# A linear-attention and SwiGLU kernel whose whole instruction order is made by the builder's detailed timeline simulation

## The chip, the cores and the metric

The kernel runs on one core of a Trainium2 chip. The metric is device time in microseconds of one execution. TensorE (PE; its weight loads are PEld), VectorE (DVE), ScalarE (ACT) and GpSimd (POOL) each work through their own instructions in the order in which the builder has put them; SyncE (SP) issues most of the DMA transfers, also in order. An instruction that waits holds up everything behind it on its engine.

## The reference, cut to what matters

The input x has 2048 rows of 576. It is normalised by row, and two branches of it are multiplied.

```python
xn = _layernorm(x)
# A: linear attention, 32 heads of 18
q, k, v = split(xn @ wqkv)
phi = lambda t: concat(softmax(t @ w_phi), softmax(-(t @ w_phi)))
o = (phi(q) @ (phi(k).T @ v)) / (phi(q) @ phi(k).sum() + 1e-6)
s = o @ wo
# B: SwiGLU with 4608 hidden columns
g = silu((silu(xn @ w_gate) * (xn @ w_up)) @ w_down)
return x + s * g
```

All of it is in float32. Times below are microseconds from the start of the span of the profiled execution.

## The kernel before, in words

Every float32 operand is split into a rounded high part (ScalarE, L60) and the rest (VectorE, L61), and a product is three matmuls, high by high, high by low and low by high, in the fp32r type. The gate and up products and the down products are made by Strassen's scheme with seven products of half-size blocks.

The kernel has these stages.

- The head (0 to about 66). Sixteen tiles of x (`xn`) are loaded by SyncE (L177), normalised (statistics L186, scaling L201 on ScalarE and L204 on VectorE), transposed on TensorE (`tp`, L216) and copied out of PSUM on ScalarE and VectorE (`X`, L218 to L224; the last copy, L224, is `xr`). The feature weights are folded (`tp`, L249). SyncE also stores sums of X to DRAM for later (`a_dram`, L337).
- The key stage (about 66 to 230): the projections of keys (`p2`) and values (`vx`, `vy`, `vw`, copied out in L429), the softmax parts (L313 to L321) and the state `kvp`.
- The query stage (about 240 to 490): sixteen query tiles (`p2`, written by `q_tile`), each with its softmax parts and denominators on VectorE (L604 to L614). For each pair of tiles `numer` works through five groups of heads: transposes into `pt` (L625), their split into `ph` and `pl`, the product with the state into `po` (L631), and its split into `oh` and `ol`; `project` multiplies these with wo into `p` (L651).
- The two main passes over the hidden columns (about 490 to 1010 and 1010 to 1580), one for each half of the rows. A unit is 128 hidden columns: seven products of seven matmuls of 512 columns each into `px`, `py` and `pw` (L758). Two snapshots of px are taken by ScalarE (`s`, L787) and added to pw by VectorE (L792) before the next product may write into the same bank. Between the products the down products (`pd`, L875, 288 columns) of earlier units are put in by calls of `fill`. Unit weights are split on the chip in pass 0 and stored to `w_dram` (L736), and read back from there in pass 1 (L732); the tail rows of the weights come from `t_dram` into two tiles in turn, `wt0` and `wt1` (L741).

Some hidden columns are treated early, by `early_tile` (`pe`, L94), as work for TensorE beside the head, the key stage and the query stage; their results (`h_dram`) are loaded again in the main passes.

What sets the order: the program text gives instructions in one order, and the builder of the tile context then lays out all engines' instructions by simulating the program with a cost for each, its dependences and priorities (`tc.high_priority`) and with the constraints of `tc.issue_after`. In the kernel before, that simulation uses a short estimate of each instruction. The ring of hand-offs in the query stage reads:

```python
for s in range(2):
    for j, e in enumerate(es):
        nc.tensor.transpose(pt[0:w, s, j * P:(j + 1) * P], e[:, s * D + o:s * D + o + w], ident)
split(ph[0:w], pl[0:w], pt[0:w])
for k, (a, p) in enumerate(((KVH, ph), (KVL, ph), (KVH, pl))):
    for s in range(2):
        nc.tensor.matmul(po[0:w], a[0:w, 2 * g + s, 0:w], p[0:w, s], start=k + s == 0, stop=k + s == 3)
split(oh[0:w, g], ol[0:w, g], po[0:w])
```

and the part of a unit with snapshots:

```python
product(xp, w, 5, S2, False, False)
s2 = snap(xp)
fill()
product(xp, w, 2, S3, False, False)
s3 = snap(xp)
add(wp, s3)
fill()
```

## Time and profile before

| what | us |
|---|---|
| median of three runs | 1603.73 |
| the runs | 1602.67 to 1605.22 |
| profiled execution | 1603.6 |
| its span, first to last instruction | 1601.7 |
| TensorE busy in the span | 1590.1 |
| VectorE busy | 1176.5 |
| ScalarE busy | 724.9 |
| GpSimd busy | 663.7 |

How to read the rows: a row of the timeline has start, length, engine, line, operation, output and inputs with sizes, the count of instructions that were merged into it, and in brackets how long the engine sat idle before it and what released it. A row of a group has its count, then busy time and the mean length of one in ns, then idle time before it with what ended it. A row of windows has the stretch, its length, then busy time (and count) of PE, PEld, DVE, ACT and POOL, the granted clock, the share of the DMA engines and GB/s. Matmuls overlap, so the time that one takes of the queue is the distance between two starts, not the length of a row.

### The profile page before, as it was taken

What the parts mean: (1) busy time and instruction counts of PE and PEld (TensorE: products, weight loads), DVE (VectorE), ACT (ScalarE), POOL (GpSimd) and SP (SyncE); (2) the same over time, 40 slices, a digit from 0 to 9 for tenths busy, and PEclk for the clock granted to TensorE, in tenths of its full rate; (3) what the DMA queues carried; (4) which work ended last, traced back from release to release, by engine and by line L of the source; (5) the groups of instructions that cost most, each with busy time, mean ns of one, the idle gap of its engine ahead of it and who ended that gap; (6) DMA issues with size and microseconds to landing.
All of it is one profiled execution on the core that took longest, in us unless ns stands there. A gap on an engine that the chain in (4) does not pass through costs nothing.

```text
span 1601.7 us, 25319 instructions
## 1 busy us (share of the span) xinstructions
PE 1590.1 (99%) x9415; PEld 1420.7 (89%) x9415; DVE 1176.5 (73%) x1729; ACT 724.9 (45%) x1404; POOL 663.7 (41%) x714
## 2 busy tenths in 40 slices
PE   9999999999999999999999999999999999999998
PEld 6899998999988888888888888888888888888887
DVE  7777769889866778987777778635667656666577
ACT  5633345444435654544444444455343333333334
POOL 3676662434115535544535445223324324133133
PEclk9999999999999999999999999999999999999999
DMA  9522243436438454455545453874545565556435
GB/s 313 189 81 80 91 145 115 126 108 189 127 132 280 164 192 165 164 180 189 179 163 201 171 180 124 325 229 139 163 138 146 183 193 158 171 181 187 143 117 178
DMA packets 123181, 268.29 MB, mean 168 GB/s; under 512 B 12978, under 2 KB 54066, under 8 KB 121778
## 3 DMA queue, kind: packets, MB, share of 16 engines
q1 hardware_dynamic: 107612, 244.73, 46.5%
q0 software_dynamic: 3552, 12.59, 2.7%
q10 hardware_dynamic: 11894, 9.35, 1.8%
q8 instruction: 74, 1.21, 0.3%
q14 instruction: 49, 0.40, 0.1%
HBM read 167.53 MB, written 99.09 MB: 166 GB/s over the span
## 4 chain that ended last, share of the span: by engine, by line
PE 92%; DVE 3%; POOL 2%; DMA 2%; ACT 1%; issue 1%; SPq 0%; ACTq 0%; DVEq 0%; POOLq 0%
PE pd L875 25%; PE px L758 24%; PE pw L758 12%; PE py L758 6%; PE p L94 6%; PE pe L94 5%; PE p L651 4%; PE kvp L330 2%; PE po L631 2%; PE vx L418 1%; PE pt L625 1%; POOL slo L363 1%; PE vy L94 1%; PE vx L94 1%; DMA wst<-in_A_w_qk 0%
## 5 line engine op out<-in xcount | busy, mean ns | idle before, releaser
L875 PEld LDWEIGHTS pd<-dw,hh 128*128 128x128 f32 x3012 | 424.0, 188 | 22.2 <-ACT pd L922 1.5
L875 PE MATMUL pd<-dw,hh 128*128 128x288 f32 x3012 | 438.5, 295 | 1.4 <-ACT pd L922 0.7
L758 PE MATMUL px<-X,w 128*128 128x512 f32 x1512 | 386.5, 390 | 0.0
L758 PEld LDWEIGHTS px<-X,w 128*128 128x128 f32 x1512 | 274.6, 188 | 49.1 <-ACT s L787 2.3
L758 PE MATMUL pw<-X,w 128*128 128x512 f32 x744 | 190.7, 392 | 0.0
L758 PEld LDWEIGHTS pw<-X,w 128*128 128x128 f32 x744 | 138.6, 188 | 29.4
L792 DVE TENSOR_TENSOR s<-pw,s 128x512 f32<-128x512 f32 x126 | 86.4, 687 | 97.7 <-ACT s L787 86.4
L1029 DVE TENSOR_TENSOR acc<-pd,acc 128x576 f32<-128x576 f32 x128 | 96.2, 753 | 76.9 <-PE pd L875 76.4
L787 ACT COPY s<-px 128x512 f32<-128x512 f32 x126 | 73.6, 584 | 156.7 <-PE px L758 156.7
L61 DVE TENSOR_TENSOR hh<-ha,hh 128x512 fp32r<-128x512 f32 x140 | 111.3, 821 | 21.8 <-ACT hh L60 21.4
L60 ACT CAST hh<-ha 128x512 fp32r<-128x512 f32 x140 | 82.7, 619 | 87.6 <-PE pd L875 74.3
L1001 POOL TENSOR_TENSOR hb<-hb 128x512 f32<-128x512 f32 x34 | 46.5, 1367 | 160.6 <-DVE hb L804 159.6
L94 PE MATMUL pe<-X,wh 128*128 128x512 f32 x340 | 107.0, 395 | 0.3 <-ACT wh L64 0.3
L61 DVE TENSOR_TENSOR w<-ld,w 128x512 fp32r<-128x512 f32 (+1 forms) x96 | 80.5, 839 | 34.2 <-ACT w L60 32.9
L758 PE MATMUL px<-X,wt 128*128 128x512 f32 x252 | 98.1, 389 | 0.0
L758 PE MATMUL py<-X,w 128*128 128x512 f32 x378 | 97.0, 391 | 0.0
L988 POOL TENSOR_TENSOR h<-ha,hb 128x512 f32<-128x512 f32 x34 | 44.6, 1313 | 124.2 <-DVE ha L808 94.1
L1014 POOL TENSOR_TENSOR ha<-ha 128x512 f32<-128x512 f32 x34 | 52.6, 1563 | 97.2 <-DVE hh L61 97.2
L60 ACT CAST w<-ld 128x512 fp32r<-128x512 f32 (+1 forms) x96 | 52.8, 550 | 87.3 <-POOL ld L746 57.2
L812 ACT COPY py<-px 128x512 f32<-128x512 f32 x63 | 36.0, 572 | 103.8 <-PE px L758 74.9
L743 POOL TENSOR_TENSOR ts<-ld 128x256 f32<-128x256 f32 x32 | 27.6, 864 | 127.0 <-issue 71.4
L758 PEld LDWEIGHTS py<-X,w 128*128 128x128 f32 x378 | 67.8, 188 | 10.7
(286 smaller groups left out, 3256.1 us busy)
## 6 DMA issues: line engine op xcount, KB each, us to landing
w_dram<-w SPq DMA_DIRECT2D x90, 512.0 KB
w<-w_dram SPq DMA_DIRECT2D x90, 512.0 KB
wt<-t_dram SPq DMA_DIRECT2D x62, 336.0 KB
ld<-in_B_w_gu SPq DMA_DIRECT2D x32, 512.0 KB
rt<-in_B_w_down SPq DMA_DIRECT2D x33, 288.0 KB
rb<-in_B_w_down SPq DMA_DIRECT2D x33, 288.0 KB
w_dram<-w SPq DMA_DIRECT2D x30, 256.0 KB
w<-w_dram SPq DMA_DIRECT2D x30, 256.0 KB
```

What stands on the lines that cost most here:

```text
L60: nc.scalar.copy(hi, src)
L61: nc.vector.tensor_sub(lo, src, hi)
L94: last = nc.tensor.matmul(ps, l, r, start=n == 0, stop=n == len(pairs) - 1)
L651: nc.tensor.matmul(ps[:, 0:HALF], a[0:w, g, jc], bw[0:w, g, n], start=k == 0, stop=k == 3 * NG - 1)
L758: nc.tensor.matmul(ps, l, r, start=first and n == 0, stop=last and n == len(mm) - 1, skip_group_check=True)
L787: snaps.append(nc.scalar.copy(t, ps))
L792: nc.vector.tensor_add(t, ps, t)
L875: nc.tensor.matmul(ps, l, r, start=first and n == 0 and m == 0, stop=n == len(hs) - 1 and m == 2, skip_group_check=True)
L988: sub(s, g["h"][0][0], g["h"][0][1])
L1001: nc.gpsimd.tensor_add(a21, a21, g["h"][1][1])
L1014: sub(a12, a12, g["h"][0][0])
L1029: nc.vector.tensor_add(a2, pd[:, :, 0:HALF], a2)
```

## The change

One argument is given to the tile context:

```diff
-    with tile.TileContext(nc) as tc:
+    with tile.TileContext(nc, schedule_with_timeline_sim=True) as tc:
```

With it the builder makes the order of every engine with its detailed timeline simulation in place of its short estimate of each instruction. What is computed, the instructions' kinds and sizes, the tiles and their buffers stay.

First place: TensorE at the end of the head. `tp_620` is the last transposed piece of x, `p2_795` the first key projection, `pe_740` an early tile. Before:

```order
L216 MATMUL tp_620<-ident_89,xn_427 128x128
L216 MATMUL tp_620<-ident_89,xn_429 128x128
L94 MATMUL pe_740<-X13_67,wh_397 128x512
L94 MATMUL pe_740<-X13_67,wl_398 128x512
L94 MATMUL pe_740<-X13_67,wh_397 128x512 x2
L94 MATMUL pe_740<-X13_67,wl_398 128x512
L94 MATMUL pe_740<-X13_67,wh_397 128x512 x2
L94 MATMUL p2_795<-KVWH_101,X10_64 128x288
```

And TensorE there now:

```order
L94 MATMUL pe_740<-X13_67,wl_398 128x512
L94 MATMUL pe_740<-X13_67,wh_397 128x512 x2
L216 MATMUL tp_609<-ident_89,xn_423 128x128
...
L216 MATMUL tp_620<-ident_89,xn_423 128x128
L216 MATMUL tp_620<-ident_89,xn_425 128x128
L216 MATMUL tp_620<-ident_89,xn_427 128x128
L216 MATMUL tp_620<-ident_89,xn_429 128x128
L94 MATMUL p2_795<-KVWH_101,X10_64 128x288
```

The early matmuls stood between the last transposes and the first key projection; now they stand ahead of the transposes. On SyncE the store of X11 to `a_dram` now stands ahead of the loads of xn_423, xn_425, xn_427 and xn_429, and was behind them; on ScalarE casts into `KVWH` (from tp_288) and `wh_275` now stand between the L218 and the L224 copies of the first block, and were behind them.

Second place: TensorE in the query stage, at the projection `p_4383` (`oh_4191` and `ol_4192` are its inputs, `po_4211` and on the products of the groups with the state). Before:

```order
L651 MATMUL p_4383<-WOH_2467,oh_4191 128x288
L651 MATMUL p_4383<-WOL_2468,oh_4191 128x288
L94 MATMUL pe_5146<-X00_60,wh_5071 128x512
L94 MATMUL pe_5146<-X01_61,wh_5071 128x512
L94 MATMUL pe_5146<-X01_61,wl_5072 128x512
L631 MATMUL po_4211<-ph_4217,KVH_2399 126x256 x2
L631 MATMUL po_4211<-ph_4217,KVL_2400 126x256 x2
L631 MATMUL po_4211<-pl_4218,KVH_2399 126x256 x2
```

And now:

```order
L651 MATMUL p_4383<-WOH_2467,oh_4191 128x288
L651 MATMUL p_4383<-WOL_2468,oh_4191 128x288
L631 MATMUL po_4211<-ph_4217,KVH_2399 126x256 x2
L631 MATMUL po_4211<-ph_4217,KVL_2400 126x256 x2
L631 MATMUL po_4211<-pl_4218,KVH_2399 126x256 x2
L651 MATMUL p_4383<-WOH_2467,ol_4192 128x288
L651 MATMUL p_4383<-WOH_2467,oh_4191 128x288
L651 MATMUL p_4383<-WOL_2468,oh_4191 128x288
L625 MATMUL pt_4462<-ident_89,e_4312 126x128
```

The early matmuls have gone from between the steps of the ring. Over the whole stage: before, early matmuls stand between the query tiles throughout, and 96 of them behind the last one (`p2_4333`); now the last of them stands ahead of the tenth tile, `p2_3529`, and the six tiles behind that one (`p2_3747`, `p2_3797`, `p2_4015`, `p2_4065`, `p2_4283`, `p2_4333`) and all groups behind them have none.

Third place: TensorE in pass 0, around the unit whose bank is `px_8386` (`px_8513` is the next unit's, `pd_8437` a down product). Before:

```order
L758 MATMUL px_8386<-X10_5247,w2_8205 128x512 x6
L758 MATMUL px_8386<-X10_5247,wt1_5223 128x512
L875 MATMUL pd_8437<-dw_8335,hh_8337 128x288 x3
L875 MATMUL pd_8437<-dw_8335,hh_8343 128x288 x3
L875 MATMUL pd_8437<-dw_8335,hh_8337 128x288 x3
L875 MATMUL pd_8437<-dw_8335,hh_8343 128x288 x3
L758 MATMUL px_8386<-X12_5252,w2_8209 128x512 x6
L758 MATMUL px_8386<-X12_5252,wt1_5223 128x512
L758 MATMUL px_8513<-X00_60,w2_8365 128x512 x4
L758 MATMUL px_8386<-X03_63,w1_8213 128x512 x6
```

And now:

```order
L758 MATMUL px_8513<-X00_60,wt0_5222 128x512
L758 MATMUL py_8387<-X01_61,w2_8196 128x512 x6
L758 MATMUL py_8387<-X01_61,wt1_5223 128x512
L758 MATMUL px_8386<-X10_5247,w2_8205 128x512 x6
L758 MATMUL px_8386<-X10_5247,wt1_5223 128x512
L758 MATMUL px_8386<-X12_5252,w2_8209 128x512 x6
L758 MATMUL px_8386<-X12_5252,wt1_5223 128x512
L758 MATMUL px_8386<-X03_63,w1_8213 128x512 x6
L758 MATMUL px_8386<-X03_63,wt1_5223 128x512
L758 MATMUL pw_8388<-X11_5257,w2_8209 128x512 x6
```

The down product and the next unit's first product no longer stand between the three px products; that first product is now done ahead of them, and down products come earlier in the pass.

## The prediction

> **What bounds the kernel now.** I read the page first, then busy time by windows, then TensorE's waits.
>
> ```profile
> span 1601.7 us, 25319 instructions
> PE 1590.1 (99%) x9415; PEld 1420.7 (89%) x9415; DVE 1176.5 (73%) x1729; ACT 724.9 (45%) x1404; POOL 663.7 (41%) x714
> PEclk9999999999999999999999999999999999999999
> PE 92%; DVE 3%; POOL 2%; DMA 2%; ACT 1%; issue 1%; SPq 0%; ACTq 0%; DVEq 0%; POOLq 0%
> ...
> 250.00:460.00 210.00, 209.96 (x1410) 191.84 (x1409) 186.57 (x293) 96.10 (x167) 58.48 (x120) 1.00 0.41 124
> 500.00:1010.00 510.00, 509.27 (x2824) 451.28 (x2823) 405.45 (x576) 255.41 (x508) 256.99 (x246) 1.00 0.51 175
> 1010.00:1580.00 570.00, 570.00 (x3140) 503.52 (x3139) 363.68 (x518) 228.01 (x444) 169.73 (x138) 1.00 0.57 177
> ...
> PE tp L216 <- DVE xn L204: 1.2, 2, 0.7
> PE p L94 <- ACT xr L224: 0.6, 1, 0.6
> ```
>
> TensorE (first figure after each window's length) is busy 1590.1 of 1601.7 us and never sits idle for long: 209.96 of 210 us in the query stage, 509.27 of 510 and 570.00 of 570 in the two main passes, at the full granted clock. Its two waits shown here are of the head. So an order can give back at most 1601.7 - 1590.1 = 11.6 us, and only if the same matmuls run as fast. What it can take away has no such bound: every product's result goes to another engine, and TensorE stays busy only because other matmuls stand in its queue meanwhile.
>
> What a hand-off needs in cover is read from one stretch of pass 0 (start, length), TensorE rows first, then the engines that read PSUM:
>
> ```profile
> 665.46 0.39 PE L758 MATMUL px<-X,wt 128*128 128x512 f32 x1
> 665.68 1.75 PE L875 MATMUL pd<-dw,hh 128*128 128x288 f32 x12
> 667.26 1.53 PE L758 MATMUL px<-X,w 128*128 128x512 f32 x6
> ...
> 665.88 0.59 ACT L787 COPY s<-px 128x512 f32<-128x512 f32 x1 [2.29 <-PE px L758]
> 670.41 0.62 ACT L60 CAST w<-ld 128x512 fp32r<-128x512 f32 x1 [0.78 <-PE pw L758]
> ...
> 688.10 0.69 DVE L792 TENSOR_TENSOR s<-pw,s 128x512 f32<-128x512 f32 x1 [0.28 <-PE pw L758]
> ```
>
> Twelve 288-column matmuls lie between 665.68 and 667.26, so one costs 0.132 us of the queue; a 512-column one costs 0.22 to 0.23 (665.46 to 665.68). ScalarE starts the copy 0.42 us after the last matmul of px started. After a release TensorE resumes about 0.05 us later: the head's row at 66.59, quoted below, follows a copy that ends at 66.54. So from one px to the next TensorE needs 0.42 + 0.59 + 0.05 - 0.23 = 0.83 us of other matmuls; for pw, with the vector add, 0.93; for px behind a weight cast, 0.86. Here 12 down matmuls, 1.58 us, give that cover.
>
> **The change part by part.** The same instructions run; only their order moves. The cost is therefore the cover that is lost, place by place. Distances below are counted in the new order as TensorE work between the producer's last matmul and the waiting matmul, at the spacings above.
>
> Head.
>
> ```profile
> 20.00:40.00 20.00, 19.56 (x111) 16.07 (x110) 19.39 (x48) 15.22 (x23) 5.60 (x12) 1.00 1.02 364
> ...
> 32.13 1.81 SPq L177 DMA_DIRECT2D xn<-in_A_x  x4
> ...
> 46.73 0.57 DVE L204 TENSOR_SCALAR xn<-xn,mv,rs 128x576 f32<-128x576 f32 x1
> ...
> 47.45 0.66 PE L216 MATMUL tp<-ident,xn 128*128 128x128 f32 x3 [0.51 <-DVE xn L204]
> 66.59 0.40 PE L94 MATMUL p<-KVWH,X 128*128 128x288 f32 x1 [0.55 <-ACT xr L224]
> ...
> 65.48 1.06 ACT L224 COPY xr<-tp 128x1024 f32<-128x1024 f32 x1
> ```
>
> The four last loads of x are issued at 32.13; what they feed is normalised from 46.73 and the key stage opens at 66.59. SyncE's new row puts the 1280 KB store of X11 ahead of these loads. At the 364 GB/s of the window that holds them it takes 3.6 us, and the loads also wait until X11 is ready. ScalarE's new row puts a KVWH cast and a wh cast ahead of the copies that free tp, and the early matmuls that stood between the last transposes and p2_795 are now ahead of the transposes: that work isn't lost, but the copies to L224 stand bare. I add 7 us (from 4, the store alone, to 11, the store twice over and the bare copies).
>
> Key stage. The v products come closer to the copies that free their bank.
>
> ```profile
> 74.25 0.44 ACT L429 COPY v<-vx 128x252 f32<-128x252 f32 x2
> 74.58 0.53 ACT L429 COPY v<-vy 128x90 f32<-128x90 f32 x3
> ```
>
> Behind two copies it needs 0.42 + 0.44 + 0.05 - 0.13 = 0.78, behind three 0.87; the new distances are 0.87 to 1.09, so only another instruction ahead on ScalarE makes a wait: 0 to 0.3 us at 16 places, 0 to 5; I take 2.
>
> Query stage. The early matmuls (pe) are this stage's filler.
>
> ```profile
> L94 PE MATMUL pe<-X,wh 128*128 128x512 f32 x174 | 55.7, 395 | 0.0
> L94 PE MATMUL pe<-X,wl 128*128 128x512 f32 x70 | 27.7, 395 | 0.0
> ...
> L313 DVE TENSOR_REDUCE m<-p 128x32 f32<-128x576 f32 x28 | 20.9, 748 | 1.2 <-PE p L94 1.2
> L61 DVE TENSOR_TENSOR pl<-pt,ph 126x512 fp32r<-126x512 f32 (+1 forms) x38 | 25.4, 685 | 5.9 <-ACT ph L60 5.7
> L61 DVE TENSOR_TENSOR ol<-po,oh 126x256 fp32r<-126x256 f32 (+1 forms) x36 | 15.1, 419 | 5.6 <-ACT oh L60 5.5
> ...
> L60 ACT CAST ph<-pt 126x512 fp32r<-126x512 f32 (+1 forms) x38 | 21.5, 588 | 24.5 <-PE pt L625 13.9 <-PE po L631 10.1
> L60 ACT CAST oh<-po 126x256 fp32r<-126x256 f32 (+1 forms) x37 | 13.7, 371 | 25.7 <-PE po L631 24.8 <-DVE pl L61 0.8
> ```
>
> These groups are of the window 250 to 460: 28 reductions at two a tile make 14 query tiles, 15.0 us of TensorE and 186.57 / 14 = 13.3 us of VectorE each. The filler is 244 matmuls x 0.228 / 14 = 4.0 us a tile, so a tile without filler has 11.0 us of TensorE against 13.3 of VectorE: VectorE becomes the bound, by 2.3 us. The new row has its last filler ahead of q tile p2_3529: the six q tiles behind that one and the groups behind them have none (before, 96 stand behind the last q tile alone). Six x 2.3 = 14 us is the lower end. From the other side, the queue in that stretch is a strict ring of projection, po, projection, pt: 17 waits of pt for pl at a distance of 0.40, where 0.42 + 0.59 + 0.69 + 0.05 - 0.11 = 1.64 is needed (0.11 estimated for a transpose from the 288-column spacing); 17 of the projection for oh at 0.13, needed 0.71; 15 of po for ol at 0.83, needed 1.13. That is 17 x 1.24 + 17 x 0.58 + 15 x 0.30 = 35 us if no wait covered another. In one group they follow each other, and a wait at one lets the next catch up; I take the middle, 24.
>
> Main passes. The first px product of the next unit is pulled ahead, and then the X10, X12 and X03 products of the same unit stand back to back with nothing between. Distances px to px: 12 at 0 and one at 0.40, short of 0.83: 10.4 us. pw behind the vector add: 7 at 0, 3 at 0.23, 5 at 0.40, 7 at 0.62, short of 0.93: 13.4 us. px behind a weight cast: 3 at 0.23 and 7 at 0.62, short of 0.86: 3.6 us. Before, none of these was under 0.79. The sum is 27; a wait just ahead shortens some, and I take 24 (14, half of it, to 34, a quarter more for vector adds that find VectorE at work).
>
> Weight loads. Before, the fold's tail weights (wt) and the w2 weights had 10 us or more between the release of their buffer and the use. In the new order 19 of the 62 wt loads have 3.0 to 4.3 us and 21 of the w2 loads 4.2 to 5.5. What a load needs is bounded by these rows of SyncE's queue and GpSimd behind it:
>
> ```profile
> 1203.90 0.33 SPq L962 DMA_DIRECT2D rb<-in_B_w_down  x1
> 1204.33 0.38 SPq L732 DMA_DIRECT2D w<-w_dram  x1
> 1204.80 0.38 SPq L741 DMA_DIRECT2D wt<-t_dram  x1
> 1205.47 0.33 SPq L962 DMA_DIRECT2D rb<-in_B_w_down  x1
> ...
> 1206.67 0.81 POOL L989 TENSOR_TENSOR td<-rb,rt 128x288 f32<-128x288 f32 x1 [0.20 <-DMA rb<-in_B_w_down]
> 1210.88 1.07 POOL L989 TENSOR_TENSOR td<-rb,rt 128x288 f32<-128x288 f32 x1 [1.64 <-DMA rb<-in_B_w_down]
> ```
>
> Alone at the front, 288 KB are there 1206.67 - 1203.90 = 2.8 us after the issue; behind a w and a wt it took 1210.88 - 1205.47 = 5.4. So a wt load costs nothing when it is alone and up to about 2 us when it queues: 0 to 40 x 0.5 = 20 us on average; nearest to the front in SyncE's new row, I take 5.
>
> The clock. TensorE's starting matmuls on zeros (31 in all) run 10 in one window and 17 in the next:
>
> ```profile
> 3.00:6.60 3.60, 3.60 (x10) 1.29 (x9) 2.06 (x6) 1.04 (x1) 0.00 (x0) 1.00 1.04 328
> 6.60:10.00 3.40, 3.40 (x17) 1.53 (x16) 2.69 (x9) 0.20 (x1) 1.74 (x5) 1.00 0.93 251
> ```
>
> That is 0.36 against 0.20 us apiece though the granted clock reads 1.00 in both. No later stretch shows such a pace. The Trainium skill, "TensorE: Matmul & The Clock Gate", Part 1: The HAM clock gate, says that idling through a window of about 3.4 us puts TensorE back to half rate until as long a busy window has passed; the rows agree for the start, and no run here shows it later. By that rule the longer pause in the head would add an estimated 2 us, a sum of 1668.
>
> Sum: 7 + 2 + 24 + 24 + 5 = 62 us on the profiled execution, 1601.7 in the span and 1603.6 with what lies around it, which is the median of the runs (1603.73). Forecast 1603.6 + 62 = 1666 us.
>
> **The rivals.**
> The cover is lost less than it looks. Waits in a chain pay once: after one, ScalarE and VectorE are ahead and the next hand-offs find them free. Then only half of the query and main terms stand, 24, with half of the rest, 7: 1635. For it speaks that ScalarE is busy 45%; against it, that px to px at distance 0 contains no queue of another engine, only 0.83 us of latency.
>
> Late weights decide. If SyncE's queue holds stores of w_dram ahead of the wt loads in pass 0, the 40 close loads cost 1 us each: 40 in place of 5, 1701. For it speaks the 5.4 us; against it, that each wait of TensorE lets the next load get ahead.
>
> Faster. The new order closes the head's waits and the last slices, where the 11.6 us of idle TensorE are, and the main loop's hand-offs keep cover: at best 1592, likely about 1596 if two thirds are closed. It decides from the point at which a px to px hand-off costs no more than what stands between: 0.23 us of cover would have to do in place of 0.83. The rows at 665.88 and 688.10 speak against it.
>
> No change, that the order is not new, is excluded by the moved rows; 1604 could come only from gains that cancel the losses.
>
> **How the numbers follow.** Forecast (1640 to 1690) 0.57; less than it looks (1612 to 1640) 0.19; late weights (above 1690) 0.11; faster 0.08; the same 0.05. About 0.2%, 3.2 us, is what a measurement of this kernel can tell from no change. Slower is 0.57 + 0.19 + 0.11 = 0.87. The unknown ends alone give 4 + 0 + 14 + 14 + 0 = 32 (1636) and 11 + 5 + 35 + 34 + 20 = 105 (1709). With the first rival's far end the range is 1620 to 1705, leaving out 0.08 + 0.05 and a few hundredths at each end.
>
> **What would show it.** Head: the first p matmul near 74 in place of 66.59. Query stage: PE busy under 85% over its last 80 us, waits of pt for pl, of the projection for oh, with none in the first half. Main passes: waits of px for ACT L787 and of pw for DVE L792 of 0.5 to 0.9 us, some tens of them, 20 us and more together. Weight loads: waits of px for DMA wt. Wrong it would be if TensorE's busy time plus these waits didn't rise by 30 us, if the loss sat in one place that I priced low (DMA above all), or if matmuls themselves became slower at unchanged distances.

## The result, and the profile after

The changed kernel took 1726.83 us (median of four runs, 1726.12 to 1728.6) beside 1603.76 us for the kernel before on the same chip: a ratio of 1.0769 (95% interval 1.0756 to 1.0782). It is slower, as forecast, but by 123 us where 62 were forecast. Its profiled execution took 1728.6 us.

The head of the page, changed kernel:

```profile
span 1726.5 us, 25329 instructions
PE 1631.2 (94%) x9415; PEld 1440.7 (83%) x9415; DVE 1187.9 (69%) x1729; ACT 725.4 (42%) x1408; POOL 671.7 (39%) x714
PEclk9999999999989999999999999999999999999999
PE 78%; DVE 12%; ACT 4%; DMA 3%; issue 2%; POOL 1%; SPq 0%; DVEq 0%; ACTq 0%; POOLq 0%
```

The counts of TensorE's and VectorE's instructions are those of before. TensorE's busy time rose by 41 us, its idle time from 11.6 to 95.3, by 84. VectorE now holds 12% of the chain that ended last, where it held 3%. The clock, 9 in every slice before, has an 8 in the slice that begins at 475.

To see where the time went I cut both spans at three places: the first matmul on KVWH, the first on QH, and the first px product (in the changed kernel, and in the runs below, at the one py matmul ahead of that product, which moves 0.2 us between the last two stages). The stages then hold the same matmuls in both kernels. First the kernel before, then the changed one (stretch, length, busy time of PE, PEld, DVE, ACT and POOL, granted clock, DMA share, GB/s):

```profile
0.00:66.59 66.59, 62.81 (x365) 48.46 (x366) 51.77 (x118) 43.20 (x60) 25.30 (x53) 1.00 0.88 290
66.59:223.31 156.72, 156.50 (x1222) 154.20 (x1223) 113.78 (x146) 58.29 (x149) 111.12 (x110) 1.00 0.26 88
223.31:484.26 260.95, 260.68 (x1696) 235.96 (x1695) 218.16 (x339) 120.60 (x205) 79.01 (x145) 1.00 0.45 139
484.26:1601.70 1117.44, 1110.13 (x6136) 982.11 (x6134) 792.75 (x1128) 502.78 (x991) 448.22 (x406) 1.00 0.54 178
```

```profile
0.00:81.83 81.83, 65.89 (x366) 51.14 (x366) 54.39 (x122) 43.59 (x60) 26.99 (x54) 0.96 0.73 239
81.83:239.59 157.76, 157.15 (x1222) 155.51 (x1223) 114.75 (x141) 56.87 (x150) 109.36 (x107) 0.99 0.25 83
239.59:551.39 311.80, 278.44 (x1694) 249.25 (x1693) 218.49 (x337) 121.41 (x206) 79.59 (x146) 0.96 0.36 110
551.39:1726.55 1175.16, 1129.77 (x6136) 984.75 (x6136) 800.24 (x1130) 503.54 (x993) 455.78 (x409) 1.00 0.53 171
```

| stage | before | after | more | forecast |
|---|---|---|---|---|
| head | 66.6 | 81.8 | 15.2 | 7 |
| key stage | 156.7 | 157.8 | 1.0 | 2 |
| query stage | 260.9 | 311.8 | 50.9 | 24 |
| main passes | 1117.4 | 1175.2 | 57.7 | 29 (24 and 5 for weight loads) |

The loss is where it was put, the key stage is right, and the three others are each about twice as large. In the query stage 33 of the 51 us are idle time of TensorE and 18 are busy time. Four other readings follow; the experiments then ask what lies behind them.

TensorE's waits, changed kernel (what waited, for what, us in total, times, longest):

```profile
PE pw L758 <- DVE s L792: 17.9, 24, 2.3
PE pt L625 <- DVE pl L61: 13.5, 13, 3.0
PE px L758 <- ACT s L787: 12.5, 14, 2.8
PE p L651 <- ACT oh L60: 11.4, 22, 0.9
PE tp L216 <- DVE xn L204: 5.2, 3, 2.7
...
PE px L758 <- DMA wt<-t_dram: 2.0, 3, 1.0
PE px L758 <- ACT w L60: 1.6, 3, 0.5
```

These are the hand-offs that the prediction named: pw behind the vector add, px behind the snapshot, pt behind pl, the projection behind oh. The waits for loaded weights are 2.4 us (2.0 for wt, shown, and 0.4 for w).

The main passes: one wait of pw, VectorE and TensorE in turn, changed kernel:

```profile
1224.72 3.02 DVE L61 TENSOR_TENSOR hh<-hb,hh 128x512 fp32r<-128x512 f32 x2 [0.69 <-ACT hh L60]
1225.36 0.39 PE L758 MATMUL pw<-X,wt 128*128 128x512 f32 x1
1225.59 1.88 PE L875 MATMUL pd<-dw,hh 128*128 128x288 f32 x13
1227.66 0.68 DVE L792 TENSOR_TENSOR s<-pw,s 128x512 f32<-128x512 f32 x1
1228.39 1.66 PE L758 MATMUL pw<-X,w 128*128 128x512 f32 x6 [0.92 <-DVE s L792]
```

Here thirteen down products do stand between the two pw products, 1.88 us, twice the 0.93 that I asked for; and TensorE still waits 0.92, because the add that it waits for stands behind two splits of hh on VectorE that end at 1227.74 (1224.72 + 3.02).

The query stage past its middle, TensorE and then VectorE, changed kernel:

```profile
406.28 0.66 PE L625 MATMUL pt<-ident,e 128*126 128x128 f32 x4 [0.42 <-DVE pl L61]
410.75 0.47 PE L625 MATMUL pt<-ident,e 128*126 128x128 f32 x1 [1.84 <-DVE pl L61]
407.47 1.36 DVE L614 TENSOR_TENSOR e<-e,y 128x1152 f32<-128x1152 f32 x1
408.75 1.34 DVE L588 TENSOR_TENSOR tl<-tl,th 128x896 f32<-128x896 f32 x1
410.01 0.68 DVE L61 TENSOR_TENSOR pl<-pt,ph 126x512 fp32r<-126x512 f32 x1
```

The ring of transpose, split, product and projection has nothing between its steps, and the short split that it turns on, 0.68 us, stands behind 2.6 us of long operations on VectorE.

The clock, four stretches of 3.41 us in the same stage, changed kernel (the granted clock is the third figure from the end):

```profile
407.27:410.68 3.41, 1.07 (x7) 0.61 (x5) 3.38 (x5) 0.85 (x2) 1.75 (x2) 1.00 0.16 63
410.68:414.09 3.41, 3.35 (x15) 3.35 (x16) 0.82 (x3) 0.99 (x2) 3.04 (x7) 0.50 0.62 148
455.06:458.47 3.41, 2.03 (x15) 1.58 (x14) 3.41 (x8) 1.54 (x3) 0.00 (x0) 1.00 0.42 125
458.47:461.88 3.41, 3.41 (x29) 3.41 (x27) 3.34 (x6) 1.43 (x3) 0.08 (x1) 1.00 0.00 0
```

After a stretch in which TensorE was busy for 1.07 of 3.41 us, the next ran at half the clock: it held 15 matmuls, and those of 288 columns start 0.24 us apart in it, where the stretch at full clock with TensorE busy throughout held 29, 0.13 apart. After one busy for 2.03 us the clock stayed whole. The changed kernel has thirteen half-clock stretches of 3.41 us, 44.4 us: two in the head, one as the key stage opens, eight in the query stage (four of them in a row, from 492.60) and two in the main passes. The kernel before has none while TensorE works; in both the record shows half clock once more at the very end, behind TensorE's last matmul.

### The profile page after: what moved, and what is told of

Read it like the earlier page. It is cut to its first block, busy times and chain, and to the rows that moved or that the text cites. A ratio compares the mean times of both kernels' runs of the same rounds, so it can differ in the third digit from the quotient of the medians.

```text
span 1726.5 us, 25329 instructions
## 1 busy us (share of the span) xinstructions
PE 1631.2 (94%) x9415; PEld 1440.7 (83%) x9415; DVE 1187.9 (69%) x1729; ACT 725.4 (42%) x1408; POOL 671.7 (39%) x714
## 4 chain that ended last, share of the span: by engine, by line
PE 78%; DVE 12%; ACT 4%; DMA 3%; issue 2%; POOL 1%; SPq 0%; DVEq 0%; ACTq 0%; POOLq 0%
PE px L758 21%; PE pd L875 19%; PE pw L758 10%; PE p L94 6%; PE py L758 6%; PE pe L94 5%; PE p L651 4%; DVE hh L61 2%; PE kvp L330 2%; DVE dw L61 2%; PE vx L418 1%; PE po L631 1%; DVE s L792 1%; DMA wt<-t_dram 1%; PE pt L625 1%
## 5 line engine op out<-in xcount | busy, mean ns | idle before, releaser
L758 PE MATMUL px<-X,w 128*128 128x512 f32 x1512 | 396.4, 395 | 15.1 <-ACT s L787 12.5
L758 PE MATMUL pw<-X,w 128*128 128x512 f32 x744 | 193.7, 396 | 17.9 <-DVE s L792 17.9
L61 DVE TENSOR_TENSOR hh<-ha,hh 128x512 fp32r<-128x512 f32 x140 | 117.4, 862 | 35.8 <-ACT hh L60 35.7
L1029 DVE TENSOR_TENSOR acc<-pd,acc 128x576 f32<-128x576 f32 x128 | 95.3, 750 | 52.5 <-PE pd L875 51.5
L61 DVE TENSOR_TENSOR w<-ld,w 128x512 fp32r<-128x512 f32 (+1 forms) x96 | 75.4, 787 | 40.3 <-ACT w L60 40.3
L94 PEld LDWEIGHTS pe<-X,wh 128*128 128x128 f32 x340 | 65.1, 193 | 21.3 <-DVE X L228 3.2
```

What stands on the lines that cost most here:

```text
L61: nc.vector.tensor_sub(lo, src, hi)
L94: last = nc.tensor.matmul(ps, l, r, start=n == 0, stop=n == len(pairs) - 1)
L758: nc.tensor.matmul(ps, l, r, start=first and n == 0, stop=last and n == len(mm) - 1, skip_group_check=True)
L1029: nc.vector.tensor_add(a2, pd[:, :, 0:HALF], a2)
```

## The experiments

Every kernel below was profiled beside the kernel before; times are medians, and stages are cut as above. (The expectations put 56 us of the loss in the query stage and 51 in the main passes; the table's cuts give 51 and 58, and it is these that I compare with.)

**A border alone, and the attention alone.** The builder can lay out a block by itself. Two kernels put all that comes before the main passes into such a block. The first keeps the short estimate in both parts, so that the border's own price is known; the second orders the block with the detailed simulation and the main passes with the short estimate.

```diff
+    with tc.block(schedule_with_timeline_sim=False):   # first kernel; True in the second
         with ExitStack() as att:
             ...
```

> Control: the short estimate throughout, but everything up to the main passes stands in a block of its own, so that nothing of the main passes is moved across that border. All theories expect the order of the kernel before but for the border: 1604 to 1615 us.

Measured: 1606.87 us, 1.0023 of before (1.0011 to 1.0035). The border costs 3.5 us; the head is 1.1, the query stage 0.9 and the main passes 2.9 us longer than without it.

> The detailed simulation only in the block up to the main passes (head, key and query stage), the short estimate in the main passes. In the changed kernel's trace the head's end is 15 us later than before, the key stage adds 1, and the query stage about 56. Every theory expects these here again and nothing in the main passes: e1 plus 72, about 1680 us (1670 to 1690). If the main passes' loss had come out of what the earlier stages left them (late loads, late early tiles), it would stay and the time be near 1727.

Measured: 1680.06 us, 1.0481 (1.0450 to 1.0511). Its query stage and main passes:

```profile
237.72:549.20 311.48, 278.14 (x1695) 248.87 (x1694) 218.70 (x337) 120.87 (x205) 79.86 (x145) 0.96 0.34 107
549.20:1678.48 1129.28, 1113.16 (x6136) 983.84 (x6136) 790.22 (x1130) 504.99 (x994) 451.78 (x409) 0.99 0.55 179
```

The query stage is that of the changed kernel, 311.5 beside 311.8, and the main passes are within 9 us of those of the kernel with the border alone (1120.4). Of these 9, one wait at the border makes 7.95: TensorE stands still until 560.84, behind a copy of px on ScalarE that stands behind the cast of weights whose load is issued only at 553.91. So the losses add up, and neither causes the other: of the 123 us, 77 come with the attention's order (the border and this wait are in them) and the other 47 with that of the main passes.

**The filler and the reserve held back.** The filler is the early matmuls of the query stage; the reserve is the next unit's first px product and the down products. The theory of the prediction (theory A) is that the cover was spent early. If so, the time must come back when the builder is kept from spending it, with its detailed simulation left on. In the query stage each early matmul from the 99th on is tied behind a step of the ring, spread over the whole stage; in the main passes the first four matmuls of the next unit's first px product are tied behind this unit's third px product, the other three behind its last product, and each down product behind the product that stands just ahead of it in the program text.

```diff
-            last = nc.tensor.matmul(ps, l, r, ...)
+            behind = pace.pop(0) if pace and not stationary_x else None
+            with tc.issue_after(behind.ins) if behind else ExitStack():
+                last = nc.tensor.matmul(ps, l, r, ...)
...
+        pace += [None] * 98 + [steps[4 + n * (len(steps) - 4) // 266] for n in range(266)]
```

> The changed kernel, with each early matmul held behind a step of the query stage so that they are spread over it as before (TensorE order alone, by issue_after). Theory A, the cover was spent early and the half-rate clock windows follow from the bare ring: the query stage's excess of 56 us falls to 10 to 20 and the granted clock stays at 1 from 400 to 570; 1685 us (1675 to 1695). Theory B, the orders of VectorE and ScalarE are what makes the ring slow: 1715 to 1727. Theory C, the clock is its own cause: the half-rate windows stay and the time is 1705 to 1715.

Measured: 1703.53 us (1699.93 and 1707.13). Query stage:

```profile
237.19:525.80 288.61, 267.78 (x1695) 241.04 (x1694) 216.30 (x336) 120.27 (x205) 80.77 (x145) 0.98 0.39 117
```

From 311.8 to 288.6: 23 of the 51 us come back, where theory A asked for about 42. (The two runs lie 7 us apart; the trace is of the faster.) The half-clock stretches fall from thirteen to six, 20.5 us, with it. The lost filler is a cause of the query stage's loss, and not the whole.

```diff
-            nc.tensor.matmul(ps, l, r, start=first and n == 0, ...)
+            mark = marks[n > 3] if marks else None
+            with tc.issue_after(mark.ins) if mark else ExitStack():
+                done[0] = nc.tensor.matmul(ps, l, r, start=first and n == 0, ...)
...
-        product(xp, w, 0, A11, True, False)
+        product(xp, w, 0, A11, True, False, (mid[0], done[0]) if mid[0] else ())
...
+                with tc.issue_after(done[0].ins):
                     three(pd[:, k, 0:HALF], ...)
```

> The changed kernel, with the next unit's first px product held behind the third px product of the unit before (its last three matmuls behind that unit's last product), and each down product behind the product that stands ahead of it in the text. By counting distances, the uncovered time of px and pw goes from 27 us to 6. Theory A, the cover was spent early: the main passes' excess of 51 us falls to 10 to 18, 1690 us (1682 to 1700). Theory B, the orders of VectorE and ScalarE make the adds late: 1712 to 1727. Theory D, late weights: 1715 to 1727 with waits for wt unchanged or more.

Measured: 1692.9 us (1692.46 and 1693.34). Main passes, and TensorE's wait for the snapshots in them (line numbers moved by four or five with the edit):

```profile
552.69:1691.57 1138.88, 1117.98 (x6136) 984.94 (x6136) 806.76 (x1130) 503.50 (x993) 453.86 (x409) 0.99 0.54 177
```

```profile
PE px L762 <- ACT s L792: 5.7, 5, 2.7
```

The waits of pw for the vector add are gone from the list, those of px for the snapshot fall from 14 to 5, and 36 of the 57.7 us come back. The time lies in the range that theory A gave. In the main passes theory A holds for the larger part.

**VectorE's order in the query stage, by one constraint.** My next theory (A') was that VectorE takes the second query tile's softmax ahead of the splits that the ring waits for. The second tile's softmax is tied behind the last split of `ol` of the pair before; once alone, once with the filler held.

```diff
-            r = softmax_parts(pq, e)...
+            with tc.issue_after(packed[0].ins) if second and packed[0] else ExitStack():
+                r = softmax_parts(pq, e)...
...
-                    split(oh[0:w, g], ol[0:w, g], po[0:w])
+                    packed[0] = split(oh[0:w, g], ol[0:w, g], po[0:w])
```

> The changed kernel, with VectorE's softmax of the second query tile of a pair held behind the last split (ol) of the numerator groups of the pair before, so that the five groups' splits stand close together as before; the early matmuls stay spent early. Counted by distances, the uncovered time of the ring goes from 37 us to 22. Theory A' (in the query stage VectorE's row costs as much as the missing filler): 56 us of excess go to 35, 1706 us (1698 to 1714). Theory A (the filler alone): 1718 to 1730.

Measured: 1727.1 us, query stage 315.1, where theory A' asked for 1706. Waits move (pt for pl falls from 13.5 to 2.8 us) and others take their place.

> e3 and e5 together: early matmuls held over the whole query stage and VectorE's splits packed. By distances the uncovered time of the ring is 5 us of 37. Theory A': the query stage's excess falls from 56 to 8 to 15 us, 1683 us (1675 to 1692), with no half-rate window left between 250 and 540. Theory A: as e3, 1700 to 1706. Theory C (the clock falls by itself): half-rate windows stay, 1692 to 1702.

Measured: 1706.68 us, query stage 291.1, no better than with the filler alone. Theory A', as I put it, falls. That this one constraint does nothing doesn't clear VectorE: it moves one tile's softmax and leaves all else of the row.

**The head.** The prediction blamed SyncE's store. The trace after says otherwise: block 3's scaling on VectorE starts late. VectorE in the kernel before, then VectorE and SyncE in the changed kernel:

```profile
28.84 1.07 DVE L204 TENSOR_SCALAR xn<-xn,mv,rs 128x576 f32<-128x576 f32 x2
```

```profile
32.32 1.06 DVE L204 TENSOR_SCALAR xn<-xn,mv,rs 128x576 f32<-128x576 f32 x2
39.48 3.78 SPq L177 DMA_DIRECT2D xn<-in_A_x  x4
```

and TensorE there, changed kernel:

```profile
37.35 0.50 PE L94 MATMUL pe<-X,wh 128*128 128x512 f32 x1 [1.92 <-ACT X L218]
38.38 1.45 PE L216 MATMUL tp<-ident,xn 128*128 128x128 f32 x7
```

The first 16 of the 24 transposes behind that scaling come 3.5 us later (33.04, not 29.56). The other eight, the last that read these tiles, come later still, at 38.38 and 42.59, where before all 24 stood together: early matmuls stand ahead of them, and the first of these waits 1.92 us for a copy. The loads that reuse the tiles go out from 39.48, not 32.13. The store of X11, which the prediction blamed, went out at 26.82, 12.7 us ahead of them. So I held back what VectorE did ahead of the scaling: the fold behind the statistics of block 3 (and, for ScalarE's casts, behind a copy of the block before), the next statistics behind the scaling itself.

```diff
-                fold(wk, KVWH[:, :, :, 0:D], KVWL[:, :, :, 0:D])
+                with tc.issue_after(xr2.ins), tc.issue_after(scaled.ins):
+                    fold(wk, KVWH[:, :, :, 0:D], KVWL[:, :, :, 0:D])
...
-                norm_stats([0, 1], xns)
+                with tc.issue_after(scales[3].ins):
+                    norm_stats([0, 1], xns)
```

> The changed kernel, in the head alone: the fold's casts and splits held behind the second block's last copy (ScalarE) and the next block's scales (VectorE), and the statistics of the last two blocks held behind the scaling of the block before. If VectorE's row (statistics and splits ahead of the next block's scaling) delayed the last loads of x and with them the head, the first key projection starts at 70 to 76 in place of 81.8 and the time is 1714 us (1708 to 1722). If it was SyncE's row (the store of X11 ahead of the loads, as the prediction had it), nothing moves: 1724 to 1730.

Measured: 1722.33 us. The head falls from 81.8 to 73.2, so 8.6 of its 15.2 us were in these operations; as ScalarE's casts of the fold were held too, the share of VectorE alone is read from a run below. The loads still go out late (38.62), since early matmuls still stand ahead of the last 16 transposes (36.01), and the rest of the head's loss stays. Of the 8.6 us only 4.5 reach the end: the query stage is 2.6 and the main passes 2.1 us longer than in the changed kernel.

**What a pause does to the clock.** The kernel before, with work added behind its end: 24 bursts of 60 matmuls of 512 columns, with pauses made by one to eight ScalarE copies. Its own work is whole.

```diff
+    for n in range(24):
+        ...
+        for m in range(60):
+            nc.tensor.matmul(ps, probe[:, 0, 0:P], fixed[:, 1], start=True, stop=True)
+        src = ps
+        for m in range(n % 8 + 1):
+            step = short("s", 3)
+            last = nc.scalar.copy(step, src)
+            src = step
```

> The kernel before, with a test behind its end that the output doesn't see: 24 bursts of 60 matmuls of 512 columns (13.7 us each at full rate), and between them pauses of TensorE of 1.2 to about 5 us in eight sizes (one to eight ScalarE copies in a chain), three of each. If a half-rate window needs a whole window of 3.4 us without any matmul, at most about 2 of the 24 pauses are followed by one, all of the three longest sizes. If a window that is busy for less than about half is enough, pauses from 1.7 us on are followed by one in about half of the cases and all pauses above 3.4 us: 15 to 20 of 24. Time about 1604 + 24 x 13.7 + 24 x 3 = 2005, and 1.7 us more for each half-rate window.

Measured: bursts with the pause ahead of each (start, length of the 60, and in brackets the pause):

```profile
1612.47 13.90 PE L1163 MATMUL px<-hh 128*128 128x512 f32 x60 [0.87 <-ACT hh L1160]
1643.98 15.49 PE L1163 MATMUL px<-hh 128*128 128x512 f32 x60 [2.17 <-ACT hh L1160]
1662.30 13.90 PE L1163 MATMUL px<-hh 128*128 128x512 f32 x60 [2.82 <-ACT hh L1160]
1679.66 16.45 PE L1163 MATMUL px<-hh 128*128 128x512 f32 x60 [3.47 <-ACT hh L1160]
```

A burst takes 13.90 us at full clock. After a pause of 2.17 us it takes 15.49, 1.6 more; after one of 2.82 us 13.90; after 3.47 us 16.45, and once 13.89. At 13 of the 23 pauses between bursts the clock was halved, fewer than the 15 to 20 that I expected, and far more than the 2 of a rule that needs an empty stretch. The length of the pause alone doesn't decide; where it falls does. (The three rounds begin 146.95 and 146.79 us apart, 43 stretches of 3.413, so the three pauses of one length fall at nearly the same place and are close to one test.) I counted in stretches of 3.413 us from any border of a half-clock stretch. In this run each stretch at full clock with TensorE busy for 1.46 us or less was followed by half clock, and none busy for 1.48 or more was. In the kernels' traces, behind their start, 1.46 us or less was always followed by half clock too, but above it the border is not sharp: 1.47 us in the kernel with all holds (from 262.01) did not set it off, and this stretch, of the changed kernel with four rows of before, did, the clock of the next being 0.50:

```profile
317.81:321.22 3.41, 2.60 (x16) 1.98 (x16) 3.28 (x4) 0.87 (x3) 0.00 (x0) 1.00 0.00 0
```

To come back took more: in the changed kernel the stretches from 496.01 and 499.43, at half clock and busy for 3.08 and 3.14 us, were each followed by another at half clock. The busy time rests on modelled ends of matmuls, and what decides above 1.46 us stays open. So the waits of the ring pay twice: once as waits, and again as slow matmuls. One such stretch costs about 1.6 us (15.49 - 13.90), as far as TensorE is the bound in it; where another engine is, it may be less.

**Which row does it.** An order consists of five rows, one for each engine. From here on rows are written down as fixed chains, one instruction behind the other, while the builder makes the rest:

```diff
+    for names in ROWS.values():
+        row = [...]          # the instructions of one engine, in the order wanted
+        for p, q in zip(row, row[1:]):
+            tc.add_manual_dep(q, p.name, DependencyInfo(NoSync, DATA), reason="pin")
```

First the changed kernel with TensorE's row of before, and then the kernel before with TensorE's row of after:

> The changed kernel with TensorE's whole row pinned to the row of the kernel before (issue order only); the detailed simulation orders the four other engines around it. Theory P (TensorE's row is the cause, the other engines follow it): 1603 to 1625 us, under a fifth of the loss left. Theory R (the other engines' rows carry half of it, as e3 to e6 suggest for the query stage): 1650 to 1690.

Measured: 1656.37 us. Query stage and main passes, then TensorE's waits in the query stage:

```profile
229.67:530.40 300.73, 273.67 (x1694) 240.84 (x1694) 222.37 (x339) 122.17 (x207) 79.51 (x145) 0.97 0.40 122
530.40:1654.62 1124.22, 1111.62 (x6137) 981.79 (x6135) 799.81 (x1128) 502.99 (x991) 450.96 (x406) 1.00 0.54 177
```

```profile
PE po L631 <- DVE ol L61: 10.2, 12, 2.8
PE pt L625 <- DVE e L614: 8.0, 1, 8.0
```

The main passes are back to within 7 us. The query stage is not: 40 of its 51 us remain although TensorE's filler stands where it stood before, and TensorE waits for VectorE.

> The kernel before with TensorE's whole row pinned to the changed kernel's; the short estimate orders the four other engines around it. Theory P: the whole loss, 1710 to 1730 us. Theory R: 1650 to 1690, since the other rows aren't those of the changed kernel.

Measured: 1729.46 us, with 303.1 us for the query stage and 1183.6 for the main passes. TensorE's row of after makes the whole loss even when the short estimate orders the four others around it.

Then the four other rows:

> The kernel before with the rows of VectorE, ScalarE, GpSimd and SyncE pinned to the changed kernel's; the short estimate orders TensorE around them. Theory P: TensorE's row can stay near that of before, 1605 to 1640. Theory R, and equally a theory in which the rows force each other: 1680 to 1740.

Measured: 1898.58 us, slower than both kernels in every stage (83.4, 182.9, 342.8, 1288.5). The rows of one order don't fit TensorE's row of another: this says how much an order is one thing, and nothing of the shares of its rows.

> The changed kernel with the rows of VectorE, ScalarE, GpSimd and SyncE pinned to those of the kernel before; the detailed simulation orders TensorE around them. Theory P: TensorE's early use of its filler stays and so does the loss, 1690 to 1730. Theory R: 1605 to 1650.

Measured: 1715.36 us: head 72.1, query stage 308.6, main passes 1173.2. With all four rows of before held, the detailed simulation's choice for TensorE alone makes nearly the whole loss of query stage and main passes, 48 and 56 us.

**TensorE and VectorE together, and VectorE alone.** If VectorE's row is the rest, then the two rows of before must bring all back, and VectorE's row alone, made by the detailed simulation between four rows of before, must bring the loss of the query stage and some of the head's.

> The changed kernel with TensorE's and VectorE's rows pinned to those of the kernel before; the detailed simulation orders ScalarE, GpSimd and SyncE. e9 (TensorE's row alone) kept 53 us, nearly all of it in the query stage (about 31), the key stage (10) and the head (6), most of it in waits for VectorE. If VectorE's row is that rest: 1604 to 1618 us. If ScalarE's or SyncE's row is: 1640 to 1656.

(By the table's cuts the run with TensorE's row kept 40 us in the query stage, none in the key stage, 6 in the head and 7 in the main passes.) Measured: 1611.33 us, 1.0054 (1.0031 to 1.0076). The main passes take 1120.9 us, and the query stage:

```profile
225.92:489.61 263.69, 261.66 (x1695) 235.73 (x1694) 217.95 (x339) 119.89 (x205) 78.96 (x145) 1.00 0.44 138
```

With these two rows all but 8 of the 123 us are gone (8.3 over the kernel before on the same chip): the rows of ScalarE, GpSimd and SyncE by the detailed simulation cost those 8 us together, spread over head, query stage and main passes.

> The changed kernel with the rows of TensorE, ScalarE, GpSimd and SyncE pinned to those of before; the detailed simulation orders VectorE alone. If VectorE's row is the rest of e9: 1640 to 1660 us. If it is the others': 1604 to 1618.

Measured: 1646.48 us. Query stage, then VectorE and TensorE at its first group:

```profile
231.93:521.44 289.51, 267.95 (x1695) 237.97 (x1694) 223.04 (x339) 120.66 (x205) 81.65 (x146) 0.98 0.41 127
```

```profile
256.65 1.50 DVE L61 TENSOR_TENSOR WOL<-oh,WOH 126x1152 fp32r<-126x1152 f32 x1
258.08 1.34 DVE L606 TENSOR_REDUCE y<-ez 128x64 f32<-128x1152 f32 x1
259.34 1.34 DVE L61 TENSOR_TENSOR WOL<-ol,WOH 126x1152 fp32r<-126x1152 f32 x1
260.61 1.34 DVE L614 TENSOR_TENSOR e<-e,y 128x1152 f32<-128x1152 f32 x1
262.10 0.66 PE L625 MATMUL pt<-ident,e 128*126 128x128 f32 x2 [8.00 <-DVE e L614]
```

VectorE's row alone costs 43 us: 29 in the query stage, 9 in the head, 6 in the main passes. The last step of the first tile's softmax, `e` at 260.61, stands behind splits of the output weights (WOL), which TensorE first reads at 289.31, and behind steps of the second tile's softmax; TensorE stands still for 8.00 us. Later in the stage the same thing happens in small. VectorE's row around one split of `ol`, in the kernel before:

```
L61 TENSOR_TENSOR pl_3182<-pt_3176,ph_3181 126x512
L321 TENSOR_REDUCE sm_3248<-e_3240 128x64
L61 TENSOR_TENSOR ol_3120<-po_3157,oh_3119 126x256
L61 TENSOR_TENSOR pl_3200<-pt_3194,ph_3199 72x512
L604 TENSOR_TENSOR ez_3250<-e_3240,zb_2401 128x1152
```

and with VectorE alone by the detailed simulation:

```
L61 TENSOR_TENSOR pl_3182<-pt_3176,ph_3181 126x512
L321 TENSOR_REDUCE sm_3248<-e_3240 128x64
L604 TENSOR_TENSOR ez_3250<-e_3240,zb_2401 128x1152
L61 TENSOR_TENSOR ol_3120<-po_3157,oh_3119 126x256
L61 TENSOR_TENSOR pl_3200<-pt_3194,ph_3199 72x512
```

Ahead of the split now stand two long operations of the softmax, `sm` and `ez`, 1.35 us each, where one stood.

**All holds together.** The changed kernel with the filler, the reserve, the softmax and the head held at once.

> The changed kernel with the holds of e3, e4, e5 and e7 together: filler spread over the query stage, VectorE's splits packed, the next unit's first product and the down products held back, the head's statistics and splits held back. If the parts add up: 1727 - 23 - 34 - 5 = 1665 us (1655 to 1675). If the holds only pay together (a wait that one removes lets another show): below 1645.

Measured: 1660.27 us, 1.0357 (1.0327 to 1.0387): query stage 290.9, main passes 1138.9, head 71.7. The gains of the single holds add up (23 + 34 + 5 from the changed kernel's 1726.8 would give 1665), and more than half of the loss is back; no kernel of this study is faster than the one before.

## Why the prediction was wrong in size and right in kind

**Right.** The direction; that an order has at most 11.6 us to give and much more to take; that query stage and main passes would carry the loss (109 of 125 us of the span); the kinds of wait, each of which is in the table after; and what makes them: with the reserve held back 36 us of the main passes' loss are gone. The key stage (2, measured 1.0, of which 0.6 are the one wait of vx for a copy of v) and the weight loads (5, of which 2.0 show as waits for `wt` and 0.4 for `w`) stayed inside their ranges. "The cover is lost less than it looks", the first rival, went the wrong way: the waits of a chain didn't pay once, they also slowed the matmuls behind them. "Faster" is out. The measured time lies above the whole range, and above the 1709 of all upper ends together: what failed is not a choice within the bounds but three of the bounds.

**Head: 7, measured 15.2.** The failed step is "SyncE's new row puts the 1280 KB store of X11 ahead of these loads", with 4 to 11 us. The row is so, but that store went out at 26.82, 12.7 us ahead of the loads, and didn't hold them. The loads were late because the transposes that free their tiles were. The first of these were late because VectorE did statistics and splits ahead of block 3's scaling (32.32 in place of 28.84): holding these back brought 8.6 us, and VectorE's row alone in an otherwise old order costs 9. The last were late because early matmuls stand ahead of them in TensorE's row, which alone costs 5.5. The term was made from the rows of TensorE, ScalarE and SyncE; VectorE's row wasn't in it, and the early matmuls moved ahead of the transposes were taken as work that isn't lost.

**Query stage: 24, measured 50.9.** Both ends of my term, 14 and 35, come from TensorE's row: filler gone from between the steps. That row alone does make the stage long (308.6 with all others as before), and holding the filler back brings 23 us. What the term left out is a second cause. VectorE's own row, with TensorE's row as before, costs 29 us by itself: 8 of them are the one wait at the first group, and some 12 are waits for short splits that stand behind other work. The two prices, 48 and 29, don't add to the 51; that both make TensorE wait at the same hand-offs is my reading. Both rows put back gave 48. Third, the clock: eight half-clock stretches in this stage make up to 13 of the 51, at an estimated 1.6 us each from the bursts; 18 of the 51 are busy time of TensorE. Idle time alone rose by 33, near the term's upper end of 35, and not the middle that I took with the reason that "a wait at one lets the next catch up"; what the runs show is that a wait can also lead to a slower next step.

**Main passes: 24, measured 57.7 with the loads.** The mechanism stands, the size was off. The px term was 10.4 + 3.6 for snapshots and weight casts; 12.5 + 1.6 are shown. The pw term was 13.4; 17.9 us of waits are shown, up to 2.3 us each, where latency alone gives 0.93: the add waits in VectorE's queue, as at 1224.72. I had that in the range ("a quarter more for vector adds that find VectorE at work") at 7 us. Idle time in these passes rose from 7.3 to 45.4 us, by 38. The other 20 us are busy time of TensorE for the same matmuls. Two half-clock stretches make an estimated 3 of them, and at some 50 waits the matmul ahead shows its whole 0.39 us, not the 0.23 that it takes inside a queue: 8 more. The other 9 us I can't name.

**Clock: nothing in the sum, estimated at up to 21.** Thirteen stretches at 1.6 us are 21, already counted in the stages above. The sum had no term for the clock; 2 us for one longer pause in the head stood beside it, from a rule. The Trainium skill, "TensorE: Matmul & The Clock Gate", Part 1: The HAM clock gate, states that TensorE falls back to half rate after at least one idle window of about 3.4 us. The runs agree with the window (3.41 us, with borders that don't move) and with the half rate (0.50). They differ on what counts as idle: in the changed kernel TensorE worked for 0.36 to 1.90 of the 3.41 us in the stretch ahead of each fall, so none was idle throughout. By the rule as written there would have been no fall at all in this kernel behind its start. Of what I named as signs of an error, "matmuls themselves became slower at unchanged distances" is the one that came true.

**What stays open.** That the 5.5 us which TensorE's row adds to the head come from the early matmuls ahead of the last transposes is read from the rows; no run moved them. Open are the 9 us of busy time in the main passes, the 21 us of their loss that stay with the reserve held back, and by which of its costs the detailed simulation comes to prefer this order, since no run changed one.

## What to carry to other kernels

An order that brings work forward as soon as it can run spends the work that hides later hand-offs; before trusting a new order, count at each hand-off the work that stands between producer and consumer, and do the same on the engine in the middle, since a short operation on the path is as late as the long ones queued ahead of it. Price a lost cover at more than its latency: TensorE pays again in half-clock stretches, here always when it was busy for 1.46 of 3.41 us or less, and sometimes when it was busy for more. When two rows of an order are bad, their prices need not add: TensorE's row alone cost 112 us of 123 and VectorE's alone 43; all four other rows put back, with TensorE's left to the detailed simulation, gave only 11. So pin rows one engine at a time, and also two at a time.

## What the runs showed of the hardware that I had not expected

TensorE's granted clock changes on a fixed grid of 3.413 us, whenever the waits begin: in the changed kernel's query stage half-clock stretches start at 410.68, 441.40 and 472.12, nine times 3.413 apart each, and the first and the last of the kernel, at 38.63 and 1700.92, lie 487 times 3.413 apart. So the length of a pause alone doesn't tell what follows: in the test a pause of 2.17 us halved the clock and one of 2.82 us did not. One stretch at half clock makes 60 matmuls of 512 columns take 15.49 us in place of 13.90. A stretch need not be empty to be followed by one: TensorE was busy for up to 1.90 of 3.41 us in those of the changed kernel.
